# Gated layer of a two-layer MLP kernel: the value product is written back to its PSUM bank, and VectorE takes the low half from there

## The chip, the cores and the metric

The kernel runs on one core of a Trainium2 chip. The metric is the device time of one execution in microseconds; the time of a version is the median of its runs.

## The reference

A short causal convolution with softmax weights gives x; then two layers follow. Shapes: 8192 rows of 192 columns, 1536 gated columns in layer 1, 2048 cosine columns in layer 2, all fp32.

```python
w = softmax(weight_gen)                       # (2, 4096, 8, 7)
x = causal_conv(x, w).reshape(8192, 192)      # 7 taps, one weight per head of 24 columns
gate = 1.0 / (1.0 + np.exp(-(x @ w_gate)))    # layer 1
x = (gate * (x @ w_val)) @ w_out
h = x @ w_in                                  # layer 2
out = (h * np.cos(h)) @ w_out2
```

## The kernel before

The 8192 rows are worked off in 16 chunks of 512. A chunk of layer 1 is 12 steps, a chunk of layer 2 is 8 steps. Layer 1 runs two chunks ahead: the order is layer 1 of chunks 0 and 1, then layer 2 of chunk 0, layer 1 of chunk 2, layer 2 of chunk 1 and so on, so that 14 chunks of layer 1 alternate with layer 2. All engines run in the order in which the program issues their work (`tc.manual_schedule()`).

Each fp32 operand of a matmul is split into a high half (rounded to the matmul's format, F32R) and a low half, the operand less its high half. Three products of halves replace one fp32 product. Matmuls use 64 rows each, and two of them run side by side on the two halves of the array.

One step of layer 1 is this, with the names of the code:

- `mm_hidden` (L413): 18 matmuls of 512 columns into two PSUM banks, the gate's (`ps[0]`) and the value's (`ps[1]`). The pool `ps_h` has four banks, so two pairs; a step's pair is the one of the step before last, and every matmul waits for the last reader of its bank.
- `out_products` / `mm_out` (L432): 10 matmuls of the high and low halves of an older step with the output weights. `OUTS` says after which hidden products they are issued: not after steps 6 and 8.
- `gate` (L515): ScalarE's sigmoid from `ps[0]` to an SBUF tile `wk`.
- `product1` (L518): VectorE multiplies `ps[1]` by `wk` into `wk`. It is put on the list `pending` and issued at the begin of the next step.
- `halves` (L553, L554): ScalarE copies `wk` to the high half `gh`, and POOL subtracts, `gl = wk - gh`. It is on `pending` too.

Between the product and the next one, `do_side` issues side work of later chunks and of the weights: convolution taps (L283) and adds (L309), softmax pieces (L237 to L251), and in the first two chunks the weight decodes (L110 to L115) with POOL's low halves of the weights (L122, L184). When a chunk of layer 2 ends, its sums `va` and `vc` (L441, L442) are read out in step 1 of the following chunk of layer 1, ahead of that step's product; in step 4 (`FINAL`) its result is transposed through a pair of the `ps_h` banks (L469). In the last step of a chunk of layer 1 (step 10 of the first) the next chunk's input is transposed through such a pair (L335).

The lines of the loop that matter here:

```python
run(pending)                       # product1 and halves of the step before
do_side(k, ...)
st.mm_hidden()
...
st.gate()
run(late)
pending.append(st.product1)
pending.append(lambda st=st: st.halves(0))
```

Layer 2 has two value tiles in a step and uses the same `halves` on ScalarE and POOL.

Of the kernel before, what the change touches and what calls it, by code (L numbers as in the profile page):

```python
# [9 lines left out]
F32 = mybir.dt.float32  # L10
F32R = mybir.dt.float32r
U32 = mybir.dt.uint32
I32 = mybir.dt.int32
AF = mybir.ActivationFunctionType
ALU = mybir.AluOpType
# [14 lines left out]
def dyn_conv_glu_cos_mlp(  # L30
# [11 lines left out]
    nc = tc.nc  # L42
# [3 lines left out]
    P = 128  # L46
# [4 lines left out]
    N = TC * P  # L51
# [27 lines left out]
    gpool = ctx.enter_context(tc.tile_pool(name="gpool", bufs=5))  # L79
# [176 lines left out]
    def load_x(c):  # L256


        t0 = (c * TC + ROT) % T
        pool, tag = (xpool, "xp") if c else (tpool, "xC")  # L260
        t = pool.tile([P, TC + PAD, D], F32, name="xp", tag=tag)
        h = PAD if c == 1 else max(0, PAD - t0)
        if h and c != 1:
            for b in range(B):
                nc.gpsimd.memset(t[b * per_batch:b * per_batch + 1, 0:h, :], 0.0)
        nc.sync.dma_start(out=t[:, h:, :], in_=xr[:, t0 - PAD + h:t0 + TC, :])
        if c == 1:
            nc.gpsimd.tensor_copy(out=t[:, 0:h, :], in_=xp[0][:, TC:TC + h, :])
        elif h:
            for b in range(B):  # L270
                p0 = b * per_batch
                nc.sync.dma_start(
                    out=t[p0 + 1:p0 + per_batch, 0:h, :], in_=xr[p0:p0 + per_batch - 1, T - h:T, :]
                )
        xp[c] = t
# [94 lines left out]
    def transpose_ops(srcs, c):  # L370

        p = banks("pt")
        for n, src in enumerate(srcs):
            transposes(p, src, n == 0, n == len(srcs) - 1)
        xt = xT[1, c] = tpool.tile([P, 2, NQ, N], F32R, name="xT", tag="xB")
        yield
        yield from split_input(xt, p, c < LEAD)
# [105 lines left out]
    class Step:  # L483
# [31 lines left out]
            nc.scalar.activation(out=self.w[0], in_=self.ps[0], func=AF.Sigmoid)  # L515

        def product1(self):
            nc.vector.tensor_tensor(out=self.w[0], in0=self.ps[1], in1=self.w[0], op=ALU.mult)  # L518

        def reduce(self):  # L520

# [51 lines left out]
    later, final = [], None  # L573
# [26 lines left out]

    def do_side(k, budget):
        i = 0
        while i < len(side):
            lo, hi, cst, fn = side[i]
            if lo > k:
                i += 1
            elif hi > k and cst > budget:
                break
            else:
                side.pop(i)  # L610
                fn()
                budget -= cst

    def chain(units):

        gens = [u.ops() for u in units]
        next(gens[0])
        for g, after in zip(gens, gens[1:] + [None]):
            next(g, None)
            if after:  # L620
                next(after)
            yield
# [9 lines left out]
    def run(ops):  # L632
        for f in ops:
            f()
        ops.clear()

    with tc.manual_schedule():
# [86 lines left out]
        inputs = {seg_start[1, c - 1] + J1 - (1 if c > 1 else AHEAD): c for c in range(1, NCH)}  # L724
# [5 lines left out]
        FINAL = 4  # L730

        waiting = []
        pending = []

        def out_products():
            q = waiting.pop(0)
            q.mm_out()
            return q if q.j == q.nj - 1 else None

        for k, st in enumerate(steps):  # L740
            layer, c, j = st.layer, st.c, st.j
            ended = None
            if layer == 1:
                run(pending)
                if j == FINAL + 1 and final:
                    next(final, None)
                    final = None
                do_side(k, 2.5 if k < J1 else 2.0 if k < seg_start[2, 1] else 0.5)
                st.mm_hidden()
                old = bool(waiting) and (waiting[0].layer, waiting[0].c) != (layer, c)  # L750
                if old or len(waiting) >= 2 and OUTS[j]:
                    ended = out_products()
                st.gate()
                run(late)
                pending.append(st.product1)
                pending.append(lambda st=st: st.halves(0))
                if ended:
                    ended.finish()
                if k in inputs:
                    c1 = inputs[k]  # L760
                    ops = transpose_ops(att[c1], c1)
                    pending.pop(0)()
                    next(ops)
                    next(ops)
                    out_products()
                    pending.pop(0)()
                    for _ in ops:
                        pass
                    out_products()
                elif j == FINAL and final:  # L770
                    pending.pop(0)()
                    next(final)
            else:
                st.mm_hidden()
                n = sum(q.layer == 1 for q in waiting)
                for _ in range(-(-n // (2 - j)) if n else len(waiting) >= 2):
                    ended = out_products() or ended
                if final and j == FINAL - 1:
                    next(final)
                st.reduce()  # L780
                run(pending)
                if ended:
                    ended.finish()
                st.cosine()
                for i, r in st.tiles_of():
                    st.product2(i, r)
                    if i == 0 or st is steps[-1]:
                        st.halves(i, r)
                    else:
                        pending.append(lambda st=st: st.halves(1))  # L790
                if final and j == FINAL - 1:
                    next(final, None)
                    final = None
                do_side(k, 0.5)
                run(late)
            if todo:
                todo.pop(0).load(nc.sync)
            waiting.append(st)
            if later and not ended:
                if next(later[0], later) is later:  # L800
                    later.pop(0)
            if layer == 1 and j == st.nj - 2 and c + 2 < NCH:
                load_x(c + 2)
                if c + 4 in group_at and group_at[c + 4] > 2:
                    load_group(group_at[c + 4], "wf")
            if layer == 2 and c == 0 and j == 5:
                load_group(2, "wf")
# [35 lines left out]
```

## Time and profile before

| | us |
|---|---|
| median of 3 runs | 1254.38 (1254.14 to 1254.55) |
| span of the profiled execution (first to last instruction) | 1252.3 |
| TensorE matmul busy | 1218.8 (97%) |
| VectorE busy | 901.0 (72%) |
| ScalarE busy | 794.2 (63%) |
| POOL busy | 712.7 (57%) |

The profiled execution is given by its span; the medians are times of other executions. In the rows PE is TensorE, DVE is VectorE, ACT is ScalarE and POOL is GpSimd. An instruction is shown from its start to its end. The next instruction of the same engine can start before that end, so the step from start to start is what an instruction takes of its engine.

### The profile page before, as it was taken

To read this page: it belongs to the slowest core of one execution; us is meant where nothing else is said; L and a number is where in the kernel's file an instruction comes from. 1 tells how busy PE (TensorE), PEld (TensorE's weight loads), DVE (VectorE), ACT (ScalarE), POOL (GpSimd) and SP (SyncE) were. 2 spreads that over 40 slices of the span, in tenths; PEclk is the share of its full clock that TensorE was granted. 3 is DMA by queue.
4 is the path that set the end of the run, shared out by engine and by line. 5 is a ranking of instruction groups with operands and counts; after the bars stand their busy time and mean duration, and the time that the engine had idled before them with its cause. 6 is when DMAs were issued, how large, how long until landed. Compare 5 with 4: busy or idle time off the path is not lost.

```text
span 1252.3 us, 26914 instructions
## 1 busy us (share of the span) xinstructions
PE 1218.8 (97%) x11056; PEld 1024.8 (82%) x11056; DVE 901.0 (72%) x1309; ACT 794.2 (63%) x1326; POOL 712.7 (57%) x531
## 2 busy tenths in 40 slices
PE   6889999999999999999999999999999999999997
PEld 5677888888888888888888888888888888888885
DVE  7966887777876676877667777775877767673585
ACT  6765856648475574856657485664847657475675
POOL 3958645647465474645637465463746547464563
PEclk8999999999999999999999999999999999999999
DMA  9902202121111211111121120212111121020010
GB/s 247 248 22 58 63 14 69 27 71 27 45 33 33 69 26 51 46 42 30 26 81 27 46 51 15 58 27 73 27 45 26 39 59 26 14 52 14 1 27 26
DMA packets 27403, 61.94 MB, mean 49 GB/s; under 512 B 2580, under 2 KB 7698, under 8 KB 27280
## 3 DMA queue, kind: packets, MB, share of 16 engines
q1 hardware_dynamic: 26368, 59.09, 17.6%
q8 instruction: 86, 1.41, 0.5%
q10 hardware_dynamic: 912, 1.13, 0.3%
q14 instruction: 37, 0.30, 0.1%
HBM read 30.33 MB, written 6.29 MB: 29 GB/s over the span
## 4 chain that ended last, share of the span: by engine, by line
PE 76%; DVE 6%; ACT 3%; issue 1%; POOL 0%; DVEq 0%; ACTq 0%
PE ph L413 42%; PE po L432 33%; DVE acc L309 2%; DVE wk L518 1%; ACT wk L515 1%; DVE wk L526 1%; ACT gh L553 1%; DVE va L442 1%; PE pt L335 1%; DVE wk L534 1%; DVE wk L543 0%; ACT wk L539 0%; ACT L539 0%; DVE wk L529 0%; ACT wk L533 0%
## 5 line engine op out<-in xcount | busy, mean ns | idle before, releaser
L554 POOL TENSOR_TENSOR gl<-wk,gh 128x512 fp32r<-128x512 f32 x446 | 606.8, 1367 | 501.5 <-ACT gh L553 392.1
L413 PE MATMUL ph<-xT,unit 64*128 64x512 f32 x5760 | 773.1, 389 | 9.7 <-DVE wk L518 4.8
L413 PEld LDWEIGHTS ph<-xT,unit 64*128 64x128 f32 x5760 | 605.5, 185 | 116.3 <-DVE wk L518 13.6
L432 PE MATMUL po<-gh,outu 64*128 64x512 f32 x2688 | 557.7, 389 | 4.2 <-ACT gh L553 1.8
L432 PE MATMUL po<-gl,outu 64*128 64x512 f32 x1792 | 470.9, 387 | 4.7 <-POOL gl L554 4.6
L432 PEld LDWEIGHTS po<-gh,outu 64*128 64x128 f32 x2688 | 406.6, 184 | 56.6 <-DVE va L442 9.0
L553 ACT ACTIVATE gh<-wk 128x512 fp32r<-128x512 f32 (+1 forms) x450 | 282.9, 629 | 257.3 <-DVE wk L518 198.2
L432 PEld LDWEIGHTS po<-gl,outu 64*128 64x128 f32 x1792 | 322.3, 184 | 36.7 <-POOL gl L554 6.7
L518 DVE TENSOR_TENSOR wk<-ph,wk 128x512 f32<-128x512 f32 x192 | 131.7, 686 | 146.3 <-ACT wk L515 138.4
L543 DVE SCALAR_TENSOR_TENSOR wk<-ph,wk 128x512 f32<-128x512 f32 (+1 forms) x258 | 167.0, 686 | 39.5 <-ACT wk L539 39.5
L539 ACT ACTIVATE wk<-wk,sin_bias 128x512 f32<-128x512 f32 (+1 forms) x258 | 171.3, 713 | 10.0 <-DVE wk L529 3.8
L515 ACT ACTIVATE wk<-ph 128x512 f32<-128x512 f32 x192 | 113.5, 591 | 57.0 <-PE ph L413 56.1
L526 DVE TENSOR_SCALAR wk<-ph 128x512 f32<-128x512 f32 x129 | 88.0, 682 | 71.5 <-PE ph L413 67.0
L533 ACT ACTIVATE wk<-ph 128x512 int32<-128x512 f32 x129 | 75.5, 585 | 78.7 <-PE ph L413 78.0
L309 DVE TENSOR_TENSOR acc<-acc,pr 128x768 f32<-128x768 f32 x78 | 102.0, 1308 | 0.4
L283 DVE TENSOR_TENSOR pr<-xp,sm 128x768 f32<-128x768 f32 x84 | 96.0, 1143 | 0.0
L529 DVE SCALAR_TENSOR_TENSOR wk<-wk,ph 128x512 f32<-128x512 f32 x129 | 88.1, 683 | 4.4
L534 DVE TENSOR_TENSOR wk<-wk,ph 128x512 f32<-128x512 int32 x129 | 87.3, 677 | 0.0
L442 DVE TENSOR_TENSOR va<-po,va 128x512 f32<-128x512 f32 x32 | 22.0, 689 | 38.7 <-PE po L432 32.5
L363 DVE TENSOR_TENSOR xT<-pt,xT 64x256 fp32r<-64x256 f32 (+1 forms) x76 | 27.3, 414 | 21.5 <-ACT xT L357 21.3
L357 ACT ACTIVATE xT<-pt 64x256 fp32r<-64x256 f32 (+1 forms) x66 | 20.4, 378 | 21.5 <-PE pt L335 21.3
L122 POOL TENSOR_TENSOR unit<-wf,unit 128x768 fp32r<-128x768 f32 (+1 forms) x11 | 22.2, 2020 | 15.8 <-ACT unit L120 15.8
(61 smaller groups left out, 511.3 us busy)
## 6 DMA issues: line engine op xcount, KB each, us to landing
xT<-xT SPq DMA_DIRECT2D x90, 256.0 KB, 3.9
xp<-in_x_dram SPq DMA_DIRECT2D x13, 960.0 KB, 4.8
out_dram<-o SPq DMA_DIRECT2D x16, 384.0 KB, 2.3
rawo<-in_moe_w_out_dram SPq DMA_DIRECT2D x7, 768.0 KB, 17.4
raw<-in_moe_w_in_dram SPq DMA_DIRECT2D x8, 384.0 KB, 17.8
raw<-in_moe_w_gate_dram SPq DMA_DIRECT2D x5, 384.0 KB, 13.6
raw<-in_moe_w_val_dram SPq DMA_DIRECT2D x4, 384.0 KB, 17.2
sm<-in_weight_gen_dram SPq DMA_DIRECT2D x3, 336.0 KB, 5.2
```

The source lines that it names most:

```text
L283: nc.vector.tensor_tensor(out=out.rearrange("p t (h g) -> p t h g", g=G), in0=xp[c][:, k:k + TC, :].rearrange("p t (h g) -> p t h g", g=G) ...
L309: nc.vector.tensor_tensor(out=acc, in0=acc, in1=last, op=ALU.add)
L413: nc.tensor.matmul(ps[i], lhsT=u.t[r, w, (s + i) % NQ, c0:c0 + P], rhs=xt[r, x, s, :], start=n == 0, stop=n == len(terms) - 1,)
L432: nc.tensor.matmul(po[2 * i + a], lhsT=w[r, d0:d0 + P], rhs=g[r], start=first and g is gh and d0 < D, stop=last and g is gl,)
L515: nc.scalar.activation(out=self.w[0], in_=self.ps[0], func=AF.Sigmoid)
L518: nc.vector.tensor_tensor(out=self.w[0], in0=self.ps[1], in1=self.w[0], op=ALU.mult)
L526: nc.vector.tensor_scalar(out=w, in0=u, scalar1=0.25, scalar2=ROUND_MAGIC, op0=ALU.add, op1=ALU.add)
L534: nc.vector.tensor_tensor(out=w, in0=w.bitcast(I32), in1=u, op=ALU.subtract)
L539: nc.scalar.activation(out=w, in_=w, func=AF.Sin, scale=-SIN_SCALE, bias=sin_bias)
L543: nc.vector.scalar_tensor_tensor(out=w, in0=self.ps[i][:, r], scalar=TWO_PI, in1=w, op0=ALU.mult, op1=ALU.mult)
L553: nc.scalar.activation(out=gh, in_=w, func=AF.Copy)
L554: eng.tensor_tensor(out=gl, in0=w, in1=gh.bitcast(F32), op=ALU.subtract)
```

## The change

In layer 1, except in the last step of a chunk, step 10 of the first chunk and step 4 where a result of layer 2 is transposed, the flag `stays` is set. Then `product1` writes into the value's PSUM bank instead of `wk`, ScalarE takes the high half from that bank, and the subtract for the low half runs on VectorE from that bank instead of on POOL. The steps without the flag work as before, POOL included. The subtracts have a list of their own, `lows`, which is run behind the first side operation of the next step, or behind all of `do_side` if there is none.

```diff
         def product1(self):
-            nc.vector.tensor_tensor(out=self.w[0], in0=self.ps[1], in1=self.w[0], op=ALU.mult)
+            self.v = self.ps[1] if self.stays else self.w[0]
+            nc.vector.tensor_tensor(out=self.v, in0=self.ps[1], in1=self.w[0], op=ALU.mult)
+
+        def high1(self):
+            self.gh = [gpool.tile([P, N], F32R, name="gh", tag="gh")]
+            nc.scalar.activation(out=self.gh[0], in_=self.v, func=AF.Copy)
+
+        def low1(self):
+            self.gl = [gpool.tile([P, N], F32R, name="gl", tag="gl")]
+            eng = nc.vector if self.stays else nc.gpsimd
+            eng.tensor_tensor(out=self.gl[0], in0=self.v, in1=self.gh[0].bitcast(F32), op=ALU.subtract)
...
     def do_side(k, budget):
         i = 0
+        first = True
         while i < len(side):
...
                 fn()
                 budget -= cst
+                if first:
+                    run(lows)
+                    first = False
+        run(lows)
...
-                pending.append(st.product1)
-                pending.append(lambda st=st: st.halves(0))
+                st.stays = not (k in inputs or j == st.nj - 1 or j == FINAL and final)
+                pending += [st.product1, st.high1]
+                lows.append(st.low1)
...
-                    pending.pop(0)()
+                    run(pending)
+                    run(lows)
```

The order of TensorE, of ScalarE and of the DMA queues stays as it was; ScalarE's high halves read `ph` where they read `wk`. The order of VectorE moves, and 161 subtracts leave POOL's.

VectorE in a steady chunk of layer 1, steps 0 to 3, before (`ph` is the value's bank, `wk` the SBUF tile, `va` and `vc` the sums of the layer-2 chunk that has ended; L283 and L309 are a tap and an add of the convolution):

```order
L518 TENSOR_TENSOR wk<-ph,wk 128x512
L283 TENSOR_TENSOR pr<-xp,sm 128x768
L237 TENSOR_REDUCE st<-sm 128x32
L442 TENSOR_TENSOR va<-po_2815,va 128x512
L442 TENSOR_TENSOR vc<-po_2816,vc 128x512
L518 TENSOR_TENSOR wk<-ph,wk 128x512
L283 TENSOR_TENSOR pr<-xp,sm 128x768
L309 TENSOR_TENSOR acc<-acc,pr 128x768
L518 TENSOR_TENSOR wk<-ph,wk 128x512
```

The same place after the change:

```order
L519 TENSOR_TENSOR ph<-ph,wk 128x512
L283 TENSOR_TENSOR pr<-xp,sm 128x768
L528 TENSOR_TENSOR gl<-ph,gh 128x512
L237 TENSOR_REDUCE st<-sm 128x32
L442 TENSOR_TENSOR va<-po_2815,va 128x512
L442 TENSOR_TENSOR vc<-po_2816,vc 128x512
L519 TENSOR_TENSOR ph<-ph,wk 128x512
L283 TENSOR_TENSOR pr<-xp,sm 128x768
L528 TENSOR_TENSOR gl<-ph,gh 128x512
L309 TENSOR_TENSOR acc<-acc,pr 128x768
L519 TENSOR_TENSOR ph<-ph,wk 128x512
```

The product writes to `ph`, and the subtract (L528) stands behind one tap; it is now the last reader of the bank.

VectorE in the second chunk, steps 0 to 2, after the change (L115 is a weight decode):

```order
L519 TENSOR_TENSOR ph<-ph,wk 128x512
L115 SCALAR_TENSOR_TENSOR wf<-wf,raw 128x768
L528 TENSOR_TENSOR gl<-ph,gh 128x512
L442 TENSOR_TENSOR va<-po_444,va 128x512
L442 TENSOR_TENSOR vc<-po_445,vc 128x512
L519 TENSOR_TENSOR ph<-ph,wk 128x512
L115 SCALAR_TENSOR_TENSOR wf<-wf,rawo 128x768
L528 TENSOR_TENSOR gl<-ph,gh 128x512
```

Before, the two rows with L528 were not there, and the subtracts stood in POOL's order between the low halves of the weights.

## Rows read from the trace of the kernel before

**Rows 1.** Windows by stage: busy us (instructions) of PE, PEld, DVE, ACT, POOL, granted clock, DMA share, GB/s.
```profile
26.00:112.00 86.00, 73.67 (x654) 57.51 (x656) 69.01 (x71) 62.11 (x97) 70.49 (x42) 0.98 0.51 120
112.00:1200.00 1088.00, 1084.01 (x9846) 917.97 (x9844) 777.45 (x1140) 684.60 (x1148) 612.84 (x462) 1.00 0.15 41
```

**Rows 2.** Groups by shape: count, busy us, mean ns, idle before and releasers.
```profile
L554 POOL TENSOR_TENSOR gl<-wk,gh 128x512 fp32r<-128x512 f32 x446 | 606.8, 1367 | 501.5 <-ACT gh L553 392.1 <-PE po L432 101.3 <-issue 6.4
```

**Rows 3.** TensorE's waits from 26 to 112 us: total us, times, longest.
```profile
PE po L432 <- POOL gl L554: 4.6, 4, 3.1
PE ph L413 <- DVE wk L518: 4.3, 6, 1.0
```

**Rows 4.** Timeline, first steps: start us, us, engine, line [idle before <- releaser].
```profile
25.54 0.67 DVE L518 TENSOR_TENSOR wk<-ph,wk 128x512 f32<-128x512 f32 x1
26.14 0.94 DVE L115 SCALAR_TENSOR_TENSOR wf<-wf,raw 128x768 uint32<-128x768 uint32 x1
...
26.27 0.96 PE L413 MATMUL ph<-xT,unit 64*128 64x512 f32 x6 [0.70 <-DVE wk L518]
```

**Rows 5.** Timeline of TensorE in a steady chunk, steps 3, 5, 6 and 7.
```profile
617.54 0.39 PE L413 MATMUL ph<-xT,unit 64*128 64x512 f32 x1
...
617.77 1.98 PE L413 MATMUL ph<-xT,unit 64*128 64x512 f32 x16
...
619.59 0.39 PE L413 MATMUL ph<-xT,unit 64*128 64x512 f32 x1
...
624.40 0.47 PE L413 MATMUL ph<-xT,unit 64*128 64x512 f32 x1
...
624.98 2.33 PE L413 MATMUL ph<-xT,unit 64*128 64x512 f32 x17
626.93 0.84 PE L432 MATMUL po<-gh,outu 64*128 64x512 f32 x4
...
628.07 4.46 PE L413 MATMUL ph<-xT,unit 64*128 64x512 f32 x36
```

**Rows 6.** Timeline of VectorE in the same chunk: products of steps 1, 4, 5, tap, add.
```profile
615.99 0.68 DVE L518 TENSOR_TENSOR wk<-ph,wk 128x512 f32<-128x512 f32 x1
616.59 0.95 DVE L283 TENSOR_TENSOR pr<-xp,sm 128x768 f32<-128x768 f32 x1
617.45 0.95 DVE L309 TENSOR_TENSOR acc<-acc,pr 128x768 f32<-128x768 f32 x1
...
624.24 0.69 DVE L518 TENSOR_TENSOR wk<-ph,wk 128x512 f32<-128x512 f32 x1 [1.30 <-ACT wk L515]
...
628.63 0.68 DVE L518 TENSOR_TENSOR wk<-ph,wk 128x512 f32<-128x512 f32 x1
```

**Rows 7.** Timeline of ScalarE in the same chunk.
```profile
616.76 0.63 ACT L553 ACTIVATE gh<-wk 128x512 fp32r<-128x512 f32 x1 [1.52 <-DVE wk L518]
...
619.79 0.60 ACT L515 ACTIVATE wk<-ph 128x512 f32<-128x512 f32 x1
...
623.57 0.58 ACT L515 ACTIVATE wk<-ph 128x512 f32<-128x512 f32 x1
```

**Rows 8.** Timeline of VectorE: a short operation from PSUM, one from SBUF alone.
```profile
626.17 0.42 DVE L477 TENSOR_TENSOR o<-pf,o 128x256 f32<-128x256 f32 x1 [0.91 <-ACT o L475]
...
714.98 0.38 DVE L240 TENSOR_TENSOR sm<-sm,st 128x224 f32<-128x224 f32 x1
```

**Rows 9.** Timeline of VectorE and TensorE in the second chunk.
```profile
80.03 0.68 DVE L518 TENSOR_TENSOR wk<-ph,wk 128x512 f32<-128x512 f32 x1
...
80.62 2.27 PE L413 MATMUL ph<-xT,unit 64*128 64x512 f32 x17
...
90.16 0.50 PE L432 MATMUL po<-gl,outu 64*128 64x512 f32 x2 [3.08 <-POOL gl L554]
...
91.03 3.75 PE L413 MATMUL ph<-xT,unit 64*128 64x512 f32 x18
```

**Rows 10.** Windows, columns as in rows 1.
```profile
90.00:98.00 8.00, 7.84 (x52) 6.25 (x52) 8.00 (x4) 3.30 (x7) 7.80 (x6) 0.79 0.05 12
```

More of the change, by code (lines that the diff above doesn't have):

```diff
@@ L733, in dyn_conv_glu_cos_mlp @@
         pending = []
+        lows = []
         def out_products():
@@ L781, in dyn_conv_glu_cos_mlp @@
                 run(pending)
+                run(lows)
                 if ended:
```

## The prediction

> **What bounds the kernel now.** I read the windows by stage first, then the groups by shape, TensorE's waits in the slow stage, and the timelines of single steps. The windows [rows 1] split the run. From 112 us on TensorE is busy for 1084.0 of 1088 us at full clock, so a wait that is added there lengthens the run by itself, and one that is taken away shortens it. From 26 to 112 us it runs only 654 matmuls in 86 us, against 9846 in 1088: at the later pace, 9.05 per us, they would need 72 us. VectorE is busy for 69.0 us of that stretch and POOL for 70.5, and this is the place with something to win. POOL's subtract, which the change moves, takes 1367 ns [rows 2]. TensorE's waits in the slow stretch [rows 3] name POOL's low half as the releaser 4 times, 4.6 us in all, and VectorE's product 6 times, 4.3 us.
>
> The rule that sets every wait below is the bank's. A step's hidden product takes two PSUM banks, and two pairs serve layer 1. The value's bank is given back when the last reader is done: now VectorE's product, afterwards VectorE's subtract. In [rows 4] the product starts at 25.54 and TensorE goes on at 26.27: 0.73 us from the start of the last reader to the matmul that waited for it.
>
> **The change part by part.**
>
> *Removed from POOL.* 161 subtracts of 1.37 us (192 steps of layer 1 less 31 that stay: step 11 of 16 chunks, step 10 of the first, step 4 of 14), 220 us of busy time. After 112 us TensorE waits for none of the remaining POOL work in these rows, so this alone is worth nothing there.
>
> *Added to VectorE.* 161 subtracts. They have one operand in PSUM and one in SBUF like the product, so I take the product's step from one start to the next, 0.60 us (615.99 to 616.59, [rows 6]): 97 us spread over 1250, and VectorE has 311 us free after 112 us. Their own busy time costs nothing; what costs is when they come.
>
> *The wait that is added.* In the order of VectorE the subtract stands behind the product and one side operation. A product is 0.60, a side operation of 768 columns 0.86 (616.59 to 617.45), so the subtract starts 1.46 behind the product. By way of ScalarE it is the same: the high half starts 0.77 behind the product (615.99, and 616.76 in [rows 7]), and a VectorE operation starts 0.67 behind the ScalarE operation that it waits for (623.57 to 624.24, [rows 6, 7]): 1.44. So the bank comes free 1.46 + 0.73 = 2.19 us after the product's start instead of 0.73.
>
> *Where that is late, in a steady chunk.* [rows 5] show steps 3 to 7. Hidden product 3 begins at 617.54, and the matmul into the value's bank 0.23 later, at 617.77. That bank is step 1's, whose product starts late, at 615.99, because the two sums of the layer-2 chunk that has just ended stand in front of it on VectorE. Now it is free at 616.72, 1.05 early. After the change it is free at 618.18, 0.41 late. A wait there costs 0.13 more than itself: hidden product 5 begins at 624.40 and gets its second bank at 624.98 instead of 624.63, 0.35 late, and the next block starts at 626.93, 2.53 after its begin, where product 3 needs 2.05 (617.54 to 619.59). So the new wait costs 0.54 and the old one at step 5 costs 0.48. The old one goes: it came from taps and adds of VectorE that POOL's subtract held up, and without them the sigmoid of step 4 follows its hidden product by 0.20 (619.59, and 619.79 in [rows 7]) and the product follows by 0.67, which is 0.07 earlier than now in spite of the 0.54. Up to step 5 the change is 0.06. Step 4 keeps POOL's subtract, so the tap behind it is held up as before, and product 5 moves only from 628.63 to 628.56. Its bank is free 2.19 later, at 630.75. Hidden product 7 follows 6 with no output product between: it begins at 628.07 + 0.06 + 2.05 and wants the bank 0.23 later, at 630.41. That is 0.34 late, with the restart 0.47. Sum of a chunk: 0.06 + 0.47 = 0.53 us. The other steps stay clear by 0.2 or more in the same reckoning. Of the 14 chunks that alternate with layer 2, the first of them has softmax work in these places, loses some POOL waits too, and I set it to nothing: 13 x 0.53 = **+6.9 us**.
>
> *The start, 26 to 112 us.* Five terms. (a) The first release: the subtract of step 0 follows a weight decode that starts at 26.14 and takes 0.86, so TensorE goes on at 27.00 + 0.73 = 27.73 instead of 26.27 [rows 4]: +1.5. (b) The second chunk's step 1 has the sums ahead of its product, which starts at 80.03 [rows 9]; its bank is free at 82.22, and hidden product 3, which begins at 80.62, wants it at 80.85: 1.4 + 0.1 = +1.5. (c) The waits for POOL's low halves, 4.6 us [rows 3], go, because those halves no longer pass POOL's queue. The longest is the 3.08 at 90.16 [rows 9], and the hidden product behind it takes 3.75 us where one at full clock takes 2.05 [rows 5]: the granted clock from 90 to 98 us is 0.79 [rows 10], and TensorE had stood still just before. With that 1.7 the term is -6.3. (d) POOL loses 21 of its subtracts here, 28.7 of 70.5 us, 41%, and the taps and decodes of VectorE collide with it that much less; 41% of the 4.3 for the product is -1.8. (e) The subtract now stands behind such a tap or decode, and POOL's weight halves still hold those up: from 90 to 98 us POOL is busy for 7.80 of 8 us [rows 10]. I count one POOL operation of 1.37 once more in TensorE's path, +1.4. The 21 subtracts also lengthen VectorE's queue by 12.6 us where 17 were free; I count nothing for that, and it is the weakest point. Sum: **-3.7**. Bounds: (d) with all of 4.3 and (e) nothing, -7.6; (c) half and (d) nothing, +1.3.
>
> *PSUM as VectorE's output.* No row shows VectorE writing to PSUM. I take nothing for it, as for reading: 256 columns with an operand in PSUM take 0.42 us, 224 columns from SBUF alone 0.38 [rows 8], and 32 columns at the rate between 256 and 512 columns, 0.26 for 256, are 0.03 of the 0.04. As bounds I keep 0.04 us less (that difference taken the other way) and 0.15 more (what 0.42 has over 256 columns at that rate). At two late places in 13 chunks that is -1.0 to +3.9 us.
> [...]
>
> *Sum.* The profiled execution has a span of 1252.3 us, 2.1 below the median of 1254.38. 1252.3 + 6.9 - 3.7 = 1255.5, and with the 2.1 **1257.6 us**, 0.26% slower. A measurement of this kernel can tell about 0.2%, 2.5 us.
>
> **The rivals.**
>
> *Faster (22%).* The wait at step 7 does not come. It hangs on 0.34 us of VectorE's queue before product 5. If the tap there slips in before POOL's subtract of step 4 instead of behind it, product 5 starts some 0.4 earlier, the bank is in time, and a chunk costs 0.06. For it: nearly all of a chunk's loss is this one margin. Against: ScalarE's high half, POOL's subtract and the tap follow each other by waits and move together. Then 13 x 0.06 = 0.8, and with the start's -3.7 to -7.6 the time is 1247.6 to 1251.5, say 1250.
>
> *Slower by much more (21%).* The longer hold becomes the rule. Where the subtract's start slips by another 0.2 us (a slower write to PSUM, or a side operation held up by POOL), step 9's bank is late too, and a chunk costs 0.53 + 3 x 0.2 = 1.1: 13 x 1.1 = 14.6, with the start 1254.4 + 14.6 - 3.7 = 1265. For it: TensorE has no slack after 112 us. Against: in the steady chunks POOL is nearly idle in layer 1 afterwards.
> [...]
>
> *It does not act (7%).* Bank waits and POOL's collisions cancel or neither lies on the path: 1254. Against it: the order shows the product's output in PSUM and the subtract on VectorE at every place.
>
> **How the numbers follow.** The forecast's own case has 50%, from 1251 to 1262 by the bounds of the start and of the PSUM write. Its part below 1251.9 is 4%, within 0.2% (to 1256.9) 22%, above 24%. Faster: 21 of the first rival and 4, 25%. No change: 1 + 22 + 7 = 30%. Slower: 24 + 21 = 45%. The range of 8 in 10 leaves out the outer halves of both rivals: 1249.5 to 1264.0; the likeliest case alone is 1251 to 1262.
>
> **What would show it.** Right: in a steady chunk the first matmul into the value's bank of hidden product 3 waits about 0.4 us for VectorE's subtract, product 5's wait is gone, product 7's second matmul waits about 0.3; a period of one chunk of each layer grows by 0.5 us; the 3.08 us wait for POOL is gone; what TensorE has done by 112 us now is done some 3 to 4 us earlier. Wrong: no wait at product 7, subtracts that start more than 1.5 us behind their product, a product into PSUM that is not about 0.69 us long, or a start that is no shorter.

## The result, and the profile after

The changed kernel takes 1262.61 us (median of four executions, 1261.61 to 1264.2), the kernel before on the same chip 1254.47 (1254.14 to 1254.71). The ratio is 1.0062, 95% interval 1.0050 to 1.0074: slower by 6.3 to 9.3 us. The profiled execution took 1261.61 us with a span of 1259.8; the span of before was 1252.3, so the two traces differ by 7.5 us, and this is the difference to be found in them. One execution of a kernel below (e9_hold_step1: 1730.13 us at a granted clock of 0.65) is in no ratio.

The first view is again the windows by stage (columns as in [rows 1]).

```profile
26.00:112.00 86.00, 74.61 (x664) 60.25 (x666) 69.72 (x92) 62.62 (x98) 43.33 (x27) 0.94 0.52 121
112.00:1200.00 1088.00, 1079.79 (x9768) 914.57 (x9766) 818.21 (x1272) 679.29 (x1138) 400.11 (x311) 1.00 0.14 40
```

POOL is busy for 27 us less in the start and 213 us less in the rest, 240 us where 220 were forecast. In the start TensorE is a little ahead (664 matmuls for 654). From 112 us on it is behind (9768 for 9846), at the same granted clock, 1.00: it waits. The waits of TensorE (total us, times, longest) name the waiting matmul and the releaser, first from 26 to 112 us, then from 112 us on.

```profile
PE ph L413 <- DVE gl L528: 9.9, 7, 2.5
PE pt L335 <- DVE gl L528: 1.3, 1, 1.3
```

```profile
PE ph L413 <- DVE gl L528: 5.1, 16, 0.9
PE po L432 <- DVE va L442: 0.5, 3, 0.2
PE ph L413 <- DVE wk L519: 0.2, 1, 0.2
```

Nearly every wait is now one of a hidden product for line 528, VectorE's subtract, the last reader of the value's bank. In the start, the 4.6 us for POOL's low half and the 4.3 us for the product of [rows 3] are both gone, and 11.2 us for the subtract stand in their place. With the waits for other things (3.9 us before, 0.6 after) TensorE waits for 12.8 us there before the change and for 11.8 after it.

A steady chunk shows one such wait in full. Timeline of TensorE after the change (start us, us, engine, line, what; in brackets idle time and releaser): steps 3, 4 and 5, and 6 with 7.

```profile
620.39 0.39 PE L413 MATMUL ph<-xT,unit 64*128 64x512 f32 x1
621.03 2.33 PE L413 MATMUL ph<-xT,unit 64*128 64x512 f32 x17 [0.25 <-DVE gl L528]
622.98 0.84 PE L432 MATMUL po<-gh,outu 64*128 64x512 f32 x4
...
627.79 0.47 PE L413 MATMUL ph<-xT,unit 64*128 64x512 f32 x1
627.98 2.33 PE L413 MATMUL ph<-xT,unit 64*128 64x512 f32 x17
629.95 0.82 PE L432 MATMUL po<-gh,outu 64*128 64x512 f32 x4
...
631.08 4.86 PE L413 MATMUL ph<-xT,unit 64*128 64x512 f32 x36
635.55 0.85 PE L432 MATMUL po<-gh,outu 64*128 64x512 f32 x4
```

And VectorE's timeline of the same chunk: sums, product, tap and subtract of step 1, then the tap, add, product and subtract around step 5.

```profile
617.63 0.69 DVE L442 TENSOR_TENSOR va<-po,va 128x512 f32<-128x512 f32 x1 [2.65 <-PE po L432]
618.24 0.68 DVE L442 TENSOR_TENSOR vc<-po,vc 128x512 f32<-128x512 f32 x1
618.83 0.69 DVE L519 TENSOR_TENSOR ph<-ph,wk 128x512 f32<-128x512 f32 x1
619.43 0.95 DVE L283 TENSOR_TENSOR pr<-xp,sm 128x768 f32<-128x768 f32 x1
620.30 0.68 DVE L528 TENSOR_TENSOR gl<-ph,gh 128x512 fp32r<-128x512 f32 x1
...
629.27 1.33 DVE L283 TENSOR_TENSOR pr<-xp,sm 128x768 f32<-128x768 f32 x1
630.52 0.94 DVE L309 TENSOR_TENSOR acc<-acc,pr 128x768 f32<-128x768 f32 x1
631.39 0.68 DVE L519 TENSOR_TENSOR ph<-ph,wk 128x512 f32<-128x512 f32 x1
632.00 0.94 DVE L283 TENSOR_TENSOR pr<-xp,sm 128x768 f32<-128x768 f32 x1
632.86 0.68 DVE L528 TENSOR_TENSOR gl<-ph,gh 128x512 fp32r<-128x512 f32 x1
```

The subtract of step 1 starts 1.47 us behind its product (618.83 to 620.30), and the matmul goes on 0.73 after that, at 621.03. It was wanted at 620.39 + 0.23 = 620.62, so it is 0.41 late; the bracket gives only the 0.25 us behind the end that is shown for the matmul before it (620.78). Hidden product 3 begins at 620.39 and the next block at 622.98, 2.59 later where [rows 5] have 2.05: 0.54 us lost. Hidden product 5 runs without a wait (2.16 to the next block; it was 2.53). Products 6 and 7, one row of 36 matmuls, take 4.86 us where [rows 5] have 4.46: 0.40 lost.

To weigh such a chunk as a whole I take the time from VectorE's first sum (line 442, `va`) of a layer-2 chunk to that of the layer-1 chunk behind it. The first sum above starts at 617.63, and the next one after the change is this:

```profile
659.36 0.68 DVE L442 TENSOR_TENSOR va<-po,va 128x512 f32<-128x512 f32 x1
```

That is 41.73 us. The same pair of before (614.78 and 655.94) is 41.16. Of the 7.5 us of the spans, 13 such chunks with the chunks of layer 2 between them give 7.1 (0.55 each on average, 0.30 to 0.80 in single ones), the first chunk that alternates with layer 2 gives 1.33 (41.02 before, 42.35 after), the chunk of layer 2 ahead of it 0.1, and the start gives back 1.0: the sums of the second chunk come at 130.94 for 131.96.

### The profile page after: what moved, and what is told of

The parts are those of the page before. It is cut to its first block, busy times and chain, and to the rows that moved or that the text cites. A ratio compares the mean times of both kernels' runs of the same rounds, so it can differ in the third digit from the quotient of the medians.

```text
span 1259.8 us, 26713 instructions
## 1 busy us (share of the span) xinstructions
PE 1222.2 (97%) x11056; PEld 1030.0 (82%) x11056; DVE 948.4 (75%) x1470; ACT 795.1 (63%) x1326; POOL 478.5 (38%) x370
## 3 DMA queue, kind: packets, MB, share of 16 engines
q10 hardware_dynamic: 912, 1.13, 0.3%
## 4 chain that ended last, share of the span: by engine, by line
PE 76%; DVE 15%; ACT 5%; issue 3%; DMA 0%; DVEq 0%; ACTq 0%
PE ph L413 41%; PE po L432 33%; DVE pr L283 2%; DVE gl L528 2%; DVE ph L519 2%; DVE wk L553 2%; ACT L549 1%; PE pt L335 1%; ACT wk L549 1%; DVE acc L309 1%; DVE wk L536 1%; DVE va L442 1%; DVE vc L442 1%; PE pf L469 1%; ACT wk L543 1%
## 5 line engine op out<-in xcount | busy, mean ns | idle before, releaser
L564 POOL TENSOR_TENSOR gl<-wk,gh 128x512 fp32r<-128x512 f32 x254 | 333.0, 1321 | 187.9 <-ACT gh L563 128.2
L528 POOL TENSOR_TENSOR gl<-wk,gh 128x512 fp32r<-128x512 f32 x31 | 40.0, 1292 | 511.9 <-ACT gh L523 511.9
L523 ACT ACTIVATE gh<-ph 128x512 fp32r<-128x512 f32 x161 | 96.5, 600 | 180.3 <-DVE ph L519 179.9
L563 ACT ACTIVATE gh<-wk 128x512 fp32r<-128x512 f32 (+1 forms) x258 | 161.4, 625 | 30.6 <-DVE wk L553 23.8
L519 DVE TENSOR_TENSOR ph<-ph,wk 128x512 f32<-128x512 f32 x161 | 111.7, 694 | 62.4 <-ACT wk L515 61.2
L528 DVE TENSOR_TENSOR gl<-ph,gh 128x512 fp32r<-128x512 f32 x161 | 110.3, 685 | 36.9 <-ACT gh L523 36.7
L283 DVE TENSOR_TENSOR pr<-xp,sm 128x768 f32<-128x768 f32 x84 | 85.7, 1021 | 0.0
L309 DVE TENSOR_TENSOR acc<-acc,pr 128x768 f32<-128x768 f32 x78 | 73.9, 947 | 0.0
```

The lines of the kernel that those rows point to most:

```text
L283: nc.vector.tensor_tensor(out=out.rearrange("p t (h g) -> p t h g", g=G), in0=xp[c][:, k:k + TC, :].rearrange("p t (h g) -> p t h g", g=G) ...
L519: nc.vector.tensor_tensor(out=self.v, in0=self.ps[1], in1=self.w[0], op=ALU.mult)
L523: nc.scalar.activation(out=self.gh[0], in_=self.v, func=AF.Copy)
L528: eng.tensor_tensor(out=self.gl[0], in0=self.v, in1=self.gh[0].bitcast(F32), op=ALU.subtract)
L563: nc.scalar.activation(out=gh, in_=w, func=AF.Copy)
L564: eng.tensor_tensor(out=gl, in0=w, in1=gh.bitcast(F32), op=ALU.subtract)
```

## The experiments

Two theories at the outset. **Theory A:** the loss is the longer hold of the value's bank, at the few steps where the bank is late already. **Theory B:** it is the 161 more operations in VectorE's queue, or their writing and reading in PSUM. Each edit below is a diff against the changed kernel, and each ratio is to the kernel before on the same chip, with its 95% interval. "Layer-1 part" is the time defined above in a steady chunk, "second sums" is when VectorE's sums of the second chunk start; both are from the profiled execution.

| kernel | us (median) | ratio to before | layer-1 part | second sums |
|---|---|---|---|---|
| before | 1254.5 | 1 | 41.17 | 131.96 |
| changed | 1262.61 | 1.0050 to 1.0074 | 41.73 | 130.94 |
| e1_sbuf | 1251.4 | 0.9954 to 0.9979 | 40.84 | 133.40 |
| e2_two_back | 1254.58 | 0.9991 to 1.0009 | 41.0 to 41.13 | 130.94 |
| e3_first_two | 1252.19 | 0.9973 to 0.9990 | 41.17 | 130.69 |
| e4_hold_alone | 1263.74 | 1.0051 to 1.0076 | 41.72 | 133.23 |
| e5_start_psum | 1250.17 | 0.9944 to 0.9969 | 40.83 | 130.91 |
| e6_four_sbuf | 1249.43 | 0.9940 to 0.9965 | 40.85 | 131.46 |
| e7_four_pool | 1250.02 | 0.9944 to 0.9969 | 40.85 | 132.60 |
| e8_low_first | 1255.68 | 0.9992 to 1.0010 | 40.84 | 137.83 |
| e9_hold_step1 | 1256.77 | 1.0003 to 1.0021 | 41.32 | 132.13 |
| e10_hold_step5 | 1258.43 | 1.0013 to 1.0034 | 41.47 | 130.68 |
| e11_hold_others | 1253.89 | 0.9981 to 1.0000 | 41.08 to 41.24 | 133.06 |
| e12_no_low_start | 1243.89 | 0.9895 to 0.9922 | 40.84 | 125.50 |

(The kernel before had medians of 1255.2 to 1255.4 beside the experiments; use the ratios.)

### The subtract on VectorE, without the hold

```diff
-            self.v = self.ps[1] if self.stays else self.w[0]
+            self.v = self.w[0]
```

> The product and the high half go back to the buffer in SBUF, the subtract stays on VectorE at its new place in the order. The value's bank is given back at the product again. Theory A (the longer hold of the bank is the loss): the waits of TensorE for VectorE's subtract at hidden products 3 and 7 (0.54 and 0.40 us a chunk) are gone, and the 0.48 us wait at hidden product 5 of the kernel before does not come back, because POOL's subtract no longer holds up the taps there; a chunk is 0.4 to 0.5 us shorter than before the change, 13 times, and the first two chunks keep the gain on POOL's waits: 1243 to 1249 us. Theory B (161 more operations in VectorE's queue are the loss): nothing of that changes, 1260 to 1263 us.

Measured: 1251.4 us, faster than before, and 11.2 under the changed kernel. This is above the 1243 to 1249 that theory A gave. All 161 subtracts are still on VectorE, so the first half of theory B, the longer queue, falls for the steady chunks; the write to PSUM is left to the next experiment. A layer-1 part is 40.84, 0.33 under before rather than 0.4 to 0.5, and no wait for the subtract is left after 112 us. But the start is worse in this trace, 133.40, against what I expected. One thing that differs there is in the groups of VectorE by line from 26 to 112 us (line, engine, what, count, busy us, mean ns, idle before), first in this kernel:

```profile
L528 DVE TENSOR_TENSOR gl<-wk,gh 128x512 fp32r<-128x512 f32 x18 | 20.2, 1123 | 1.2 <-ACT gh L523 1.2
L283 DVE TENSOR_TENSOR prs<-xp,sm 128x768 f32<-128x768 f32 x8 | 15.5, 1940 | 0.0
```

and in the changed kernel:

```profile
L528 DVE TENSOR_TENSOR gl<-ph,gh 128x512 fp32r<-128x512 f32 x20 | 13.7, 683 | 1.9 <-ACT gh L523 1.9
L283 DVE TENSOR_TENSOR prs<-xp,sm 128x768 f32<-128x768 f32 x8 | 11.3, 1407 | 0.0
```

The same subtract takes 1123 ns with both operands in SBUF and 683 with one in PSUM, in the stage where POOL prepares weights; from 220 us on it takes 687 and 686. So in these two traces the subtract with an operand in PSUM stays short where POOL is busy, and the one from SBUF alone does not; what makes the difference is not shown, nor that it makes the start shorter. 1.5 of the 2.5 us by which the sums are later here than in the changed kernel come where TensorE transposes the second chunk's input, behind a wait of 1.39 us: from 60.84 it needs 7.17 us to the next hidden product, at a granted clock of 0.62 from 60.5 to 65 us, and in the changed kernel 5.65, at 1.00. And e4_hold_alone (next), whose subtract keeps its 683 ns, has its second sums at 133.23.

### The hold, without the write to PSUM

```diff
-            self.v = self.ps[1] if self.stays else self.w[0]
+            self.v = self.w[0]
...
+            if self.stays:
+                nc.vector.scalar_tensor_tensor(
+                    out=self.gl[0], in0=self.ps[1], scalar=0.0, in1=self.gh[0].bitcast(F32),
+                    op0=ALU.mult, op1=ALU.mult
+                )
```

> Product and high half in SBUF as in e1_sbuf; VectorE's operation for the low half reads the value's PSUM bank, so that the bank is held as long as in the changed kernel, while nothing is written to PSUM by VectorE. It leaves the low half of the gated values out (it is zero). Theory A (hold): as the changed kernel, 1259 to 1264 us. If it is the write to PSUM, or ScalarE's reading there, that costs: as e1_sbuf, near 1247. Theory B (queue) says 1260 to 1263 for both this one and e1_sbuf.

Measured: 1263.74 us, and 41.72 a chunk: the changed kernel's loss to 0.01, with nothing written to PSUM by VectorE. The two groups that matter, from 220 to 1200 us in this kernel, are these:

```profile
L519 DVE TENSOR_TENSOR wk<-ph,wk 128x512 f32<-128x512 f32 x156 | 107.2, 687 | 65.3 <-ACT wk L515 61.5 <-POOL gl L570 2.7
L529 DVE SCALAR_TENSOR_TENSOR gl<-ph,gh 128x512 fp32r<-128x512 f32 x130 | 89.2, 686 | 34.1 <-ACT gh L523 34.1
```

In the changed kernel the product into PSUM has a mean of 694 ns in that stretch. The write costs 7 ns, and the hold is the whole loss of a steady chunk.

### Which banks: two steps back, and one step at a time

Two steps go back to the old way from the third chunk on:

```diff
-                st.stays = not (k in inputs or j == st.nj - 1 or j == FINAL and final)
+                st.stays = not (k in inputs or j == st.nj - 1 or j == FINAL and final or c >= LEAD and j in (1, 5))
```

> From the third chunk on, steps 1 and 5 alone go back to the old way (product in SBUF, POOL's subtract); the other steps keep the new one. Theory A: these are the two banks that come late, so the waits at hidden products 3 and 7 go, 0.94 us in each of 13 steady chunks, 12 us less than the changed kernel: 1250 us, and if POOL's subtract of step 1 brings back the 0.48 us wait at hidden product 5, 1256.5. Theory B (VectorE's queue): 2 of 10 subtracts leave VectorE in each of 14 chunks, a fifth of the steady loss of 7 us, about 1261 us.

Measured: 1254.58 us, between the two figures of theory A (1250 and 1256.5) and 6 us under that of theory B. The wait at hidden product 5, which was to give the 1256.5, does not come back. The steady chunks gain 0.6 to 0.7 of the 0.94 us; what holds back the rest is hidden product 4 (below). The first chunk that alternates loses another 0.9 (43.24), which I have not traced to a step.

The cleaner test starts from e5_start_psum (below), whose steady chunks hold no bank longer and take 40.83, and puts the value back in PSUM at single steps. `psum` decides where the product goes; the subtract stays on VectorE.

```diff
-            self.v = self.ps[1] if self.stays else self.w[0]
+            self.v = self.ps[1] if self.stays and self.psum else self.w[0]
...
+                st.psum = c < LEAD or j == 1
```

> e5_start_psum (1250.2 us) with the value back in PSUM at step 1 of the third and every later chunk, and at no other step of them. Theory A: this bank is the one that hidden product 3 finds 0.4 us late, 0.54 us a chunk, 14 times: 1257.7 us. Rival (what costs is the hold at every step together, or a longer wait moves into a gap that is there anyway): under 1253 us.

Measured: 1256.77 us; 41.32 a chunk, +0.49. One held bank out of ten costs about half of the whole loss. Then `j == 5`:

```diff
+                st.psum = c < LEAD or j == 5
```

> e5_start_psum with the value back in PSUM at step 5 of the third and every later chunk alone. Theory A: hidden product 7 finds this bank late, 0.40 us a chunk, 13 or 14 times: 1255.6 us. Rival (step 5's product comes late only because step 3's wait moved TensorE against VectorE; alone it is in time): 1250 us.

Measured: 1258.43 us; 41.47 a chunk, +0.64, more than the 0.40 expected. TensorE in a steady chunk of it: hidden products 6 and 7, and the next block.

```profile
628.18 0.39 PE L413 MATMUL ph<-xT,unit 64*128 64x512 f32 x1
628.41 2.21 PE L413 MATMUL ph<-xT,unit 64*128 64x512 f32 x18
630.95 2.36 PE L413 MATMUL ph<-xT,unit 64*128 64x512 f32 x17 [0.33 <-DVE gl L528]
632.93 0.85 PE L432 MATMUL po<-gh,outu 64*128 64x512 f32 x4
```

Hidden product 6 begins at 628.18, so 7 would begin at 630.23 and want its second bank at 630.46; it gets it at 630.95, 0.49 late, and with the 0.13 of the restart that is 0.62. Together the two steps would be 1.13, and the changed kernel loses 0.90 over this base: after the wait at product 3 TensorE itself is later, and product 7 finds its bank less late. Then every step but these two, from the fourth chunk on:

```diff
+                st.psum = c < LEAD or c > LEAD and j not in (1, 5)
```

> e5_start_psum with the value back in PSUM at every step that the change moves except 1 and 5, from the fourth chunk on. Theory A: eight more banks are held 1.5 us longer in each of 13 chunks and none of them is late, so nothing is lost: 1250.2 us, within 0.7. Rival (each longer hold costs a little, the write or the read in PSUM included): 8 of 10 steps carry most of the 0.9 us of a chunk, 1257 us or more.

Measured: 1253.89 us, which neither column has: 41.08 to 41.24 a chunk, +0.25 to +0.41. In the trace the eight banks do not each cost a little; one is late. Hidden products 3 and 4 of a steady chunk here, and VectorE's subtract of step 2:

```profile
618.34 2.42 PE L413 MATMUL ph<-xT,unit 64*128 64x512 f32 x18
621.51 2.74 PE L413 MATMUL ph<-xT,unit 64*128 64x512 f32 x18
...
621.17 0.68 DVE L528 TENSOR_TENSOR gl<-ph,gh 128x512 fp32r<-128x512 f32 x1
```

In e5_start_psum both take 2.42. Hidden product 4, 0.32 longer here, uses step 2's bank: it is free at 621.17 + 0.73 = 621.90, 0.16 after it is wanted (621.74), and with the restart that is 0.29. In the changed kernel that lateness is hidden behind the wait at product 3, and in e2_two_back, which took only that wait away, it came out (2.66 in this place).

### The start and the rest apart

The new way in the first two chunks alone:

```diff
-                st.stays = not (k in inputs or j == st.nj - 1 or j == FINAL and final)
+                st.stays = c < LEAD and not (k in inputs or j == st.nj - 1 or j == FINAL and final)
```

> The new way in the first two chunks alone; from the third on everything as before the change. Both theories keep the start as in the changed kernel. If the traces are read rightly, the start gains 1.0 us and the loss lies from 131 us on (1.3 in the first chunk that alternates, 0.55 in 13 others): 1253.4 us, that is 1.0 under the kernel before. Rival: the start of the profiled execution is not typical, or its end state shifts what follows; then 1256 or more.

Measured: 1252.19 us, ratio 0.9973 to 0.9990: in the first two chunks the change is a gain of 1.3 to 3.4 us, 1.3 by the trace. The whole loss lies behind them. Now the start of the changed kernel and the steady chunks of e1_sbuf together:

```diff
+                st.psum = c < LEAD
```

> The value goes back to PSUM in the first two chunks alone; from the third on product and high half stay in SBUF and VectorE subtracts there, as in e1_sbuf. If the two halves of the run add up as the chunk periods say (e3_first_two at 1252.2, and from 131 us on 41.17 - 40.85 = 0.32 us less in 13 chunks and 0.2 in the first that alternates): 1247.8 us, under both kernels. If the gain of e1_sbuf depends on its own start: 1250 or more.

Measured: 1250.17 us, ratio 0.9956: this version beats the kernel before by 3.9 to 7.0 us and the changed one by some 12. In microseconds 1250.17 is 2.4 over the forecast of 1247.8 and just what the rival said (1250 or more). As a ratio the forecast holds: e3_first_two is 0.9982 of the kernel before, 2.3 us, and with the 4.4 of the chunks that is 6.6 us under it, inside the interval. The trace settles it: the steady chunks take 40.83 as in e1_sbuf, behind the start of the changed kernel (130.91), so the gain does not depend on e1_sbuf's start.

### What sets the pace of the start

The three longest waits for banks in the start of the changed kernel are these, of TensorE's timeline. The edits below aim at them and at one of 1.23 at 82.14 (shown below); two others, 1.34 of the transposes at 60.47 and 1.63 at 107.53, are left alone.

```profile
27.65 3.91 PE L413 MATMUL ph<-xT,unit 64*128 64x512 f32 x17 [2.14 <-DVE gl L528]
50.16 4.43 PE L413 MATMUL ph<-xT,unit 64*128 64x512 f32 x35 [1.80 <-DVE gl L528]
98.76 3.58 PE L413 MATMUL ph<-xT,unit 64*128 64x512 f32 x17 [2.52 <-DVE gl L528]
```

The hidden products behind three of the four take 3.58 to 3.91 us, where 17 matmuls take 2.33 in a steady chunk. Three kernels, each e5_start_psum with one more edit, aim at these waits. Four of the steps without the hold:

```diff
+                st.psum = c < LEAD and (c, j) not in ((0, 0), (0, 6), (1, 1), (1, 5))
```

> As e5_start_psum, with product and high half in SBUF in four more steps: 0 and 6 of the first chunk, 1 and 5 of the second, whose banks are given back late in the changed kernel (waits of 2.14, 1.80, 1.23 and 2.52 us, three of them followed by a hidden product at half the clock, 1.5 to 1.9 us longer). Theory A (the hold costs the start too): up to 7.7 + 5.2 us less; with what VectorE's queue leaves of it (e1_sbuf still waits 0.7, 0.5 and 1.1 us for the product in such places) 1240 to 1244 us. Rival (the subtract from SBUF is held up by POOL, 1.12 us instead of 0.68 as in the start of e1_sbuf, and the queue behind it with it): 1246 to 1250 us.

Measured: 1249.43 us, second sums at 131.46: no gain there. The same four on POOL:

```diff
+                st.stays = not (k in inputs or j == st.nj - 1 or j == FINAL and final or (c, j) in ((0, 0), (0, 6), (1, 1), (1, 5)))
```

> As e5_start_psum, with the same four steps back on POOL altogether (product in SBUF, POOL's subtract). Theory A: the four bank waits go as in e6_four_sbuf, VectorE's queue is shorter by four subtracts: 1239 to 1245 us. Rival: POOL's queue takes back what the change had won (TensorE waits for POOL's low half again, 1 to 3 us each): 1248 us or more.

Measured: 1250.02 us, second sums at 132.60. And the subtract directly behind the product:

```diff
-                lows.append(st.low1)
+                (pending if c < LEAD and st.stays else lows).append(st.low1)
```

> As e5_start_psum, with VectorE's subtract of the first two chunks directly behind the product instead of behind a tap or a decode: the bank is held 1.4 us + 0.7 whatever POOL does to the tap. Theory A (the hold, stretched by a tap or decode that POOL holds up, costs the start): the waits of 2.14, 1.80, 1.23 and 2.52 us shrink to under 1 us each and with them the clock drops: 1241 to 1245 us. Rival (VectorE's queue is what is full: it stands still 0.77 us for the high half each time, 20 times, 15 us where it has 17 free): 1248 to 1255 us.

Measured: 1255.68 us, 137.83, 6.9 us later than e5_start_psum. Theory A, as these expectations put it, falls for the start in all three: the rivals' figures hold in the first two, and the third is 0.7 us over its rival's. The waits that these edits aim at go or shrink, and others come: in e6_four_sbuf the wait of 2.14 becomes 0.69 and that of 2.52 one of 1.69 for ScalarE's gate, but others of 1.27, 1.90, 1.84 and 1.69 for the subtract come (at 36.45, 52.79, 86.58 and 103.87). Then e5_start_psum without the subtract itself in the start:

```diff
+            if self.stays and self.c < LEAD:
+                self.gl = [self.gh[0][:, 0:N]]
+                return
```

> e5_start_psum without VectorE's subtract in the first two chunks: the output product reads the high half in the low half's place, so the low half of the gated values is left out there. It takes some 20 operations of 0.6 us, 12 us, out of VectorE's queue of the start, and the bank is given back by ScalarE's high half. Theory V (what bounds the start is VectorE's queue, and TensorE's slower clock there costs nothing): the sums of the second chunk come at 118 to 125 us instead of 130.9, 1238 to 1244 us. Rival C (TensorE's clock drops and its own work set the start): 2 to 4 us less, 1246 to 1248. Rival D (the arrival of the weights sets the start, transfers take all DMA queues until 66 us): no change, 1250.

Measured: 1243.89 us; second sums at 125.50, 5.4 us earlier. That is just outside the 118 to 125 of theory V, whose range for the time it meets; rivals C and D fall. VectorE's busy time from 26 to 112 us, with the other engines (columns as in [rows 1]), falls in this kernel to

```profile
26.00:112.00 86.00, 77.08 (x718) 60.93 (x720) 62.62 (x73) 63.91 (x100) 45.00 (x27) 1.00 0.52 131
```

from 69.73 in e5_start_psum, and TensorE does 718 matmuls where it did 664. The granted clock is 1.00 there and 0.98 in e5_start_psum, too little between them for 5.4 us. So some 20 subtracts on VectorE cost 5.4 us in the start, by their time in its queue and by the hold together. This experiment takes both away and doesn't part them; e8_low_first, where VectorE is busy for only 57.86 us because it stands still for the high halves (0.66 to 1.17 us each), speaks for the queue, but not cleanly: its granted clock there is 0.91, so part of its 6.9 us can be the clock's.

What a fall of TensorE's clock costs there depends on what follows. Pairs of executions of one program show it: the changed kernel, e5_start_psum and e9_hold_step1 are the same up to the second sums. In the changed kernel, in the second chunk:

```profile
82.14 3.90 PE L413 MATMUL ph<-xT,unit 64*128 64x512 f32 x17 [1.23 <-DVE gl L528]
86.83 2.42 PE L413 MATMUL ph<-xT,unit 64*128 64x512 f32 x18
90.03 0.39 PE L413 MATMUL ph<-xT,unit 64*128 64x512 f32 x1
90.73 2.34 PE L413 MATMUL ph<-xT,unit 64*128 64x512 f32 x17 [0.31 <-DVE gl L528]
```

and in e5_start_psum:

```profile
82.22 2.33 PE L413 MATMUL ph<-xT,unit 64*128 64x512 f32 x17 [1.22 <-DVE gl L528]
...
86.05 2.36 PE L413 MATMUL ph<-xT,unit 64*128 64x512 f32 x17 [0.36 <-DVE gl L528]
...
90.79 2.35 PE L413 MATMUL ph<-xT,unit 64*128 64x512 f32 x17 [1.23 <-DVE gl L528]
```

The 1.6 us that the slow product costs in the first come back as longer waits in the second, and both go on within 0.06 us of each other at 90.7, and reach the second sums at 130.94 and 130.91. Here the slow product costs nothing.

At the last wait of the second chunk it does. In e5_start_psum:

```profile
107.53 2.33 PE L413 MATMUL ph<-xT,unit 64*128 64x512 f32 x17 [1.85 <-DVE gl L528]
...
110.61 2.42 PE L413 MATMUL ph<-xT,unit 64*128 64x512 f32 x18
```

and in e9_hold_step1:

```profile
107.13 3.91 PE L413 MATMUL ph<-xT,unit 64*128 64x512 f32 x17 [1.85 <-DVE gl L528]
...
111.81 2.43 PE L413 MATMUL ph<-xT,unit 64*128 64x512 f32 x18
```

From 107 to 112 us the granted clock is 1.00 in the first and 0.66 in the second, after the same wait. From this product to the next one it is 3.08 us in the first and 4.68 in the second, and no wait for VectorE follows that could take up the 1.60: e9_hold_step1, 0.40 ahead before it, has its second sums 1.22 later (132.13). In e11_hold_others and e4_hold_alone the same product takes 4.69 and 4.67 us.

## Why the prediction was right or wrong

The direction and the range were right; the time was 5.0 us too low (1257.6 for 1262.6). Of these, 2.7 are the start, 1.3 the first chunk that alternates, 0.3 the other chunks, and 0.7 that the median lies 2.8 us over the span and not 2.1. The range held partly by luck: 1262.6 lies outside the 1251 to 1262 that the prediction gives its own case, and the outer range has it only for the half of "Slower by much more" that it takes in. The 1251 to 1262 is also not what the bounds give: with the PSUM write they run from 1257.6 - 3.9 - 1.0 = 1252.7 to 1257.6 + 5.0 + 3.9 = 1266.5.

- **The rule of the bank, right.** The subtract starts 1.47 us behind its product (1.46 forecast), the matmul 0.73 behind that, and e4_hold_alone shows the hold as the cause.
- **The steady chunk, right in size and place.** 0.53 forecast, 0.55 measured; 0.54 at hidden product 3 as reckoned, the old wait at 5 gone (0.37 for the 0.48), and 0.40 at products 6 and 7 for the 0.47. "The other steps stay clear by 0.2 or more" holds only beside the wait at product 3: without that wait step 2's bank is late (e11_hold_others). What had held VectorE up ahead of hidden product 5 shows in its adds (line 309, 220 to 1200 us): 1308 ns on average before, 2.04 us at 620.29 beside POOL's subtract (619.81 to 621.53), and 948 ns now.
- **The first chunk that alternates, wrong.** I "set it to nothing"; it cost 1.33. TensorE's timeline there has three waits for the subtract, the first just ahead of the mark; two rows of ScalarE stand before them:

```profile
160.38 0.77 ACT L242 ACTIVATE sm<-sm 128x672 f32<-128x672 f32 x1 [1.41 <-DVE sm L240]
...
162.46 0.60 ACT L515 ACTIVATE wk<-ph 128x512 f32<-128x512 f32 x1
...
165.26 2.35 PE L413 MATMUL ph<-xT,unit 64*128 64x512 f32 x17 [0.86 <-DVE gl L528]
169.09 2.33 PE L413 MATMUL ph<-xT,unit 64*128 64x512 f32 x17 [0.34 <-DVE gl L528]
187.51 2.34 PE L413 MATMUL ph<-xT,unit 64*128 64x512 f32 x17 [0.34 <-DVE gl L528]
```

  I took the softmax work in these places for a reason to count nothing, but gate and product stand behind it. For the first wait, the longest, it is on ScalarE: step 0's sigmoid starts at 162.46, behind the softmax exponential (L242), and so its product at 163.09 and its subtract at 164.52, while hidden product 2 begins at 164.02. For the second it is as in a steady chunk: two reductions at 165.12, then the sums, then the product at 166.91. e5_start_psum, without the hold, takes 40.83 in this part.
- **The start, mis-sized.** -3.7 forecast, -1.0 in the trace, -1.3 to -3.4 by the runs of e3_first_two; by 112 us TensorE is 10 matmuls ahead, 1.1 us at 9.05 per us, and not 3 to 4. Terms (a) and (b) came as reckoned: TensorE goes on at 27.65 (forecast 27.73), and in the second chunk the matmul at 82.14 is 1.39 late by the starts (forecast 1.4; the bracket gives 1.23). Of term (c) the 4.6 us of waits went, but its 1.7 for the slow clock was no gain: slow products came back in other places (granted clock 0.94 in the start for the 0.98 of before). The 1.7 also sets a length that is shown, 3.75, against a step from start to start, 2.05; by the starts the slow product takes 3.58 (91.03 to 94.61), 1.5 more. And the traces above show that such a product costs nothing where the next wait takes it up. What failed is the sentence "I count nothing for that, and it is the weakest point", on VectorE's longer queue: taking the subtracts out there, the hold with them, is worth 5.4 us. New waits of 1.80 and 2.52 come where a tap of 2.26 (47.25) and a decode of 3.36 us (94.75), beside operations of POOL (46.85 to 48.69, and 93.37 to 97.29 without a break), stand ahead of the subtract; term (e) had one such case, 1.4. How the 2.7 us between forecast and trace divide between the clock, these waits and the queue, no run shows.
- **The write to PSUM, right.** Taken as nothing; from 220 to 1200 us a product takes 694 ns with it (changed kernel) and 687 without (e4_hold_alone).
- **The rivals.** "Slower by much more" had the time (1265) nearly right and its mechanism only in the first alternating chunk: a steady chunk costs 0.55, not 1.1. "Faster" fell at its own condition, the tap at 629.27 still takes 1.33 beside POOL's subtract (628.49 to 629.79). "It does not act" fell: the ratio is clear of 1.

The sum with the measured terms is 1252.3 + 7.1 + 1.33 + 0.1 - 1.0 = 1259.8, the span.

## What to carry to other kernels

Before a result is left in a PSUM bank for one more reader, find for each user of the banks when the next matmul wants it and when the last reader will be done. Ten banks a chunk were held 1.5 us longer, and two or three of them made the whole loss. Moving the same subtract to VectorE with its input in SBUF gave a gain instead (e1_sbuf). Where POOL is busy the subtract itself is shorter with the operand in PSUM (683 ns for 1123), but that this shortens the start is not shown: e5_start_psum, which takes each form in its stage, has 0.9944 to 0.9969 of the time before, and e1_sbuf 0.9954 to 0.9979. Where two waits lie in one chain, taking one away shows the next, so single edits do not add up (0.49 + 0.64 for 0.90).

## What was unexpected of the hardware

- The subtract with both operands in SBUF slowed down beside POOL and the one with an operand in PSUM did not (1123 and 683 ns, in the start). The decode at 94.75, SBUF alone, took 3.36 us beside POOL (93.37 to 97.29); the one at 50.63, with POOL idle from 50 to 52 us, took 0.94.
- ScalarE's high half takes 600 ns from PSUM and 630 from SBUF (means of 130 and 26 of them from 220 us on, in the changed kernel).
- After the same wait of 1.2 us the hidden product took 3.90 us in one execution (granted clock 0.57 from 82 to 86 us, 0.50 from 83 to 85) and 2.33 in another (1.00 from 82 to 86), with the same program up to there. A wait of 1.80 us at 50.16 was followed by products at a granted clock of 1.00 (50 to 55 us). In these traces the length of the wait alone does not tell whether the clock falls.
- The start varies between executions of the same program more than the rest does: the second sums came at 130.7 to 130.9 in five profiled executions that share the changed kernel's first two chunks, and at 132.1 and 133.1 in two more (e9_hold_step1, e11_hold_others). In these two the product behind the last wait of the second chunk was 1.6 us longer (granted clock 0.66 from 107 to 112 us in e9_hold_step1), and in the five it was not (1.00 in the changed kernel and in e5_start_psum). The changed kernel's own times may hold the same two cases (1261.61 twice, one of them the profiled execution, and 1263.61 and 1264.2), but the later two have no trace. A gain of 1 us there can't be read from one trace; that is also the spread in which e6_four_sbuf and e7_four_pool lie, and e8_low_first and e12_no_low_start lie outside it.
